# Fourier layer and two expert layers: both halves of an inverse-transform group in one burst at the end of expert steps 1 to 9

## The chip, the cores and the metric

The kernel runs on one core of a Trainium2 chip. Five engines with queues of their own work side by side: TensorE (PE, its weight loads shown as PEld), VectorE (DVE), ScalarE (ACT), GpSimd (POOL) and SyncE (SP, which issues the DMA transfers). Each takes its instructions in the order of its queue, and semaphores hold an instruction back until what it needs is there. The metric is the device time of a run in microseconds (us). The kernel before takes 1156.77 us (median of 3 runs, 1155.72 to 1156.81).

## The reference

Three layers follow each other on two sequences of 3008 tokens with 256 channels:

```python
X = np.fft.rfft(x, axis=1)                       # forward transform along the tokens
Yr = Xr @ w_r - Xi @ w_i + b_r                   # complex product with 256 x 256 weights
Yi = Xr @ w_i + Xi @ w_r + b_i
Yr = sign(Yr) * max(|Yr| - 0.01, 0)              # the same for Yi
y  = np.fft.irfft(Yr + 1j * Yi, n=3008, axis=1)  # inverse transform, 6016 x 256
h = y @ moe_w_in;   g = h * cos(h);              z   = g @ moe_w_out    # 256 -> 2048 -> 256
h = z @ moe2_w_in;  g = h * relu6(h + 3) / 6;    out = g @ moe2_w_out
```

## The kernel before, in words

The first 160 us are the forward transform, the complex product and the shrinking. The inverse transform is cut into 16 groups of 4 token pairs, 376 tokens each; a group has two halves of 128 output channels, and a half (`y_mm`, line 393) is four products of 96 rows, 128 columns of weights (`u_sb`) and 94 columns (`tg_sb`) into one PSUM bank, which the profile counts as 8 matmuls since they are in plain f32. `y_out` (lines 408 and 412) copies the bank to SBUF with ACT and stores it; after the second half it issues the loads of the next group's `u_sb` and `tg_sb`, whose buffers are single. Six groups are done during the transform stage; one follows in the drain of that stage, one half at a time, and the other nine (7 to 15) lie in the expert steps 1 to 9.

The expert layers run in 96 steps (`for k in range(2 * G)`): 6 blocks of up to 1024 tokens times 8 steps for each of the two layers. A step takes two times 128 of the 2048 hidden channels for two halves of the tokens, with the Strassen-Winograd scheme: seven products in place of eight, each product three matmuls of 512 columns (`three`, line 845), since operands are held as a high and a low part. The four results a, b, c and d stand in four PSUM banks with the tags `h0` to `h3`; a is always in `h0` and c always in `h2`. In the order of PE a step is: product A11 into a, an output group, products into c, b, a (A12), an output group, products S3 into b and S4 into d, an output group, product A22 into b, an output group. An output group (`out_mm`) multiplies one finished block's `gh` and `gl` by the output weights and adds into two accumulators, one for each half `d` of the output channels, with three matmuls each. The list `waiting` holds the blocks; the group behind A11 is that of a block of two steps ago.

Between the products stand the elementwise steps of a block (`Block`). In the first layer `first` is an ACT copy to integers (line 820) and a DVE multiply-add that reads the bank (line 821), `second` is ACT's Sin (line 829) and a DVE multiply with the bank as one operand (line 830), and `split` is an ACT copy to `gh` (line 836) and a POOL subtraction to `gl` (line 172). Line 830 is the last reader of a block's bank. DVE also adds into d and c (line 857); the copies of lines 982 and 991 are ACT's. In the steps up to 7 DVE and POOL convert the 64-bit weights of the second layer beside this, one piece at a time, at three places of a step (`other`; lines 199 to 214, 274), and the next block's operands are made with ACT and POOL (`advance`; lines 448 to 454). In steps 2 to 7 and 10 to 15 `advance` also stands between `be.first()` and `bc.second()`.

The order on each engine is the order of the code (manual schedule). What the change touches are `out_mm` and the places of the two halves in a step: the first half is issued behind the third output group into bank `h0` (`y_begin`), its copy comes at once in ACT's order (`y_end`), the second half stands behind A22, also in `h0`, and its copy behind `be.first()`.

Of the kernel before, what the change touches and what calls it, by code (L numbers as in the profile page):

```python
# [9 lines left out]
F32 = mybir.dt.float32  # L10
# [31 lines left out]
STEPS = NFC // 2  # L42
# [80 lines left out]
def fourier_moe_moe_kernel(ctx, tc, x, w_r, w_i, b_r, b_i, ta, tg, fg, win1, wout1, win2, wout2, out):  # L123
# [676 lines left out]
    with tc.manual_schedule(engines=engines):  # L800
# [57 lines left out]

        def out_mm(blk):
            m, jj, q, n = blk.m, blk.jj, blk.q, blk.n  # L860
            f = 4 * (q // 2) + q % 2 + 2 * (1 - blk.f)
            if (jj, blk.t) not in acc:
                acc[jj, blk.t] = [psum.tile([128, 512], F32, tag=f"acc{d}", bufs=2, name=f"acc{jj}_{blk.t}{d}") for d in range(2)]
            w = wo_sb[m, f // 2]
            for d in range(2):
                wz = [w[:, z, f % 2, d * 128 : (d + 1) * 128] for z in range(2)]
                three(acc[jj, blk.t][d], wz, blk.g, q == 0 and blk.f == 0, q == STEPS - 1 and blk.f == 1, n)
            if q == STEPS - 1 and blk.f == 1:
                ended.append((jj, blk.t))
# [81 lines left out]

        def y_begin(tag=None):
            if y_late:
                y_open.append(y_late.pop(0))
                name = f"yp{y_open[0][0]}_{y_open[0][1]}"
                y_mm(*y_open[0], bank(0, name) if tag is None else psum.tile([128, 512], F32, tag=tag, bufs=2, name=name))

        def y_end():
            if y_open:
                y_out(*y_open.pop())  # L960

# [11 lines left out]
        for k in range(2 * G):  # L973
# [4 lines left out]
            def mm(h, w, x, start=False):  # L978
                three(h, weights(k, w), tokens(k, x), start, True, n)

            mm(a, A11, B11, True)
            act.activation(b[:, :n], a[:, :n], AF.Copy)  # L982
            if old:
                od, oe, oc = old
                od.split()
                oe.second()
            drained(k)
            out_next(5)
            mm(c, S1, T1, True)
# [38 lines left out]
            out_next()  # L1028
            if k:
                y_begin()  # L1030
                y_end()
            bd.second()
            if k == 0:
                bc.second()
            mm(b, A22, T4)
            if k:
                y_begin()
            else:
                drained(k)
            be.first()  # L1040
            y_end()
            advance(k, False)
# [4 lines left out]
            other(k, 2)  # L1047
            ba.split()
            flush()
            old = bd, be, bc  # L1050
# [55 lines left out]
```

## Time and profile before

| | |
|---|---|
| median of 3 runs | 1156.77 us |
| span of the profiled execution | 1154.4 us |
| PE busy | 1146.0 us, 99% |
| DVE, ACT, POOL busy | 759.1, 818.3, 805.1 us |
| granted TensorE clock | 1.000 of full speed over the span |
| instructions | 15875 |

The profiled execution's own time is its span: the 1154.4 us from its first to its last instruction. The median of the timed runs is 2.4 us above that. A step's place in the trace is found by its first matmuls into `ha`: steps 1 to 10 begin at 168.01, 181.58, 194.00, 207.01, 219.17, 231.57, 244.85, 256.99, 269.12 and 281.43 us. The rows name tiles without their numbers; `yp` is the bank of a half, `yo` its copy, `ha` to `hd` are the banks of the blocks, `acc` the accumulators. A matmul of 512 columns is shown with 0.39 us, but the next begins 0.22 to 0.23 us after it: matmuls overlap, so starts are compared.

### The profile page before, as it was taken

Reading aid. Unit: us, or ns where it says so; the run is one execution under the profiler, and the core shown is the slowest. Engines: PE = TensorE matmul, PEld = TensorE weight load, DVE = VectorE, ACT = ScalarE, POOL = GpSimd, SP = SyncE. Lnnn points to the kernel's source line nnn. Section 1 sums busy time; section 2 is a strip of 40 time slices with the busy share of each in tenths; the row PEclk is TensorE's granted clock in tenths of the full one; section 3 lists DMA queues with packets and bytes.
Section 4 is the critical chain, followed back from the end, with each engine's and each line's share of the span. In section 5 each row is a group of like instructions: output and inputs, shape, how many; then the busy total and the mean of one; then the engine's idle time right before and its main releaser. Section 6 shows DMA issues by size and latency. Waiting matters only on the chain.

```text
span 1154.4 us, 15875 instructions
## 1 busy us (share of the span) xinstructions
PE 1146.0 (99%) x5345; PEld 961.7 (83%) x5345; DVE 759.1 (66%) x1096; ACT 818.3 (71%) x1561; POOL 805.1 (70%) x650
## 2 busy tenths in 40 slices
PE   9999999999999999999999999999999999999998
PEld 7888877878888888888889987888888888888897
DVE  5888867876988788889886677643443433433443
ACT  5787787777888878888888875565566565556554
POOL 3556747876886996897877776557667667567544
PEclk9999999999999999999999999999999999999999
DMA  9656858435113113112025310020020010100100
GB/s 241 179 149 176 260 173 308 145 109 183 55 37 110 46 55 110 37 73 100 34 63 211 137 69 1 1 74 1 1 73 1 29 45 1 69 1 1 37 1 32
DMA packets 48450, 98.94 MB, mean 86 GB/s; under 512 B 6240, under 2 KB 23184, under 8 KB 47728
## 3 DMA queue, kind: packets, MB, share of 16 engines
q1 hardware_dynamic: 48096, 97.66, 26.3%
q8 instruction: 42, 0.69, 0.2%
q14 instruction: 40, 0.33, 0.1%
q10 hardware_dynamic: 272, 0.26, 0.1%
HBM read 59.76 MB, written 38.14 MB: 85 GB/s over the span
## 4 chain that ended last, share of the span: by engine, by line
PE 95%; DVE 2%; ACT 1%; issue 1%; POOL 1%; DVEq 0%; ACTq 0%; POOLq 0%
PE acc L845 43%; PE hb L845 16%; PE ha L845 11%; PE pp L630 6%; PE hc L845 5%; PE hd L845 5%; PE bp L659 3%; PE yp L393 3%; PE zp L533 2%; PE vp L695 1%; DVE r L830 0%; ACT r L829 0%; POOL x_big L552 0%; POOL tok L451 0%; DVE hd L857 0%
## 5 line engine op out<-in xcount | busy, mean ns | idle before, releaser
L172 POOL TENSOR_TENSOR gl<-r,gh 128x512 fp32r<-128x512 f32 (+1 forms) x382 | 498.1, 1320 | 254.1 <-ACT gh L836 237.6
L845 PE MATMUL acc<-gh,wo 128*128 128x512 f32 (+1 forms) x1536 | 529.5, 386 | 0.0
L845 PEld LDWEIGHTS acc<-gh,wo 128*128 128x128 f32 x1536 | 288.4, 188 | 53.5
L845 PE MATMUL acc<-gl,wo 128*128 128x512 f32 (+1 forms) x768 | 296.3, 386 | 0.0
L845 PE MATMUL hb<-tok,wi 128*128 128x512 f32 (+1 forms) x864 | 241.2, 387 | 2.0 <-ACT hb L982 0.7
L836 ACT ACTIVATE gh<-r 128x512 fp32r<-128x512 f32 (+1 forms) x384 | 227.5, 614 | 1.6 <-DVE r L830 1.2
L845 PEld LDWEIGHTS hb<-tok,wi 128*128 128x128 f32 x864 | 160.9, 188 | 34.0 <-DVE hc L857 1.7
L857 DVE TENSOR_TENSOR hd<-p,hb 128x512 f32<-128x512 f32 (+1 forms) x96 | 65.8, 685 | 159.6 <-PE hb L845 152.6
L845 PEld LDWEIGHTS acc<-gl,wo 128*128 128x128 f32 x768 | 144.2, 188 | 27.8 <-POOL gl L172 1.1
L829 ACT ACTIVATE r<-r 128x512 f32<-128x512 f32 (+1 forms) x192 | 118.7, 618 | 58.4 <-DVE r L821 58.4
L845 PE MATMUL ha<-tok,wi 128*128 128x512 f32 (+1 forms) x576 | 159.8, 386 | 0.0
L845 PEld LDWEIGHTS ha<-tok,wi 128*128 128x128 f32 x576 | 108.0, 188 | 20.5 <-ACT r L829 0.3
L451 POOL TENSOR_TENSOR tok<-st,tok 128x512 fp32r<-128x512 f32 (+1 forms) x77 | 98.6, 1292 | 3.4 <-ACT tok L448 3.4
L991 ACT ACTIVATE p<-hc 128x512 f32<-128x512 f32 (+1 forms) x96 | 56.5, 588 | 54.3 <-PE hc L845 54.1
L823 ACT ACTIVATE r<-hd 128x512 f32<-128x512 f32 (+1 forms) x48 | 28.4, 591 | 78.3 <-PE hd L845 78.3
L845 PE MATMUL hc<-tok,wi 128*128 128x512 f32 (+1 forms) x288 | 79.9, 386 | 0.0
L845 PE MATMUL hd<-tok,wi 128*128 128x512 f32 (+1 forms) x288 | 79.7, 385 | 0.0
L982 ACT ACTIVATE hb<-ha 128x512 f32<-128x512 f32 (+1 forms) x96 | 55.3, 576 | 31.9 <-PE ha L845 31.5
L857 DVE TENSOR_TENSOR hc<-p,hb 128x512 f32<-128x512 f32 (+1 forms) x96 | 65.3, 681 | 16.1 <-PE hb L845 15.3
L845 PEld LDWEIGHTS hc<-tok,wi 128*128 128x128 f32 x288 | 53.9, 188 | 10.5 <-DVE r L830 0.4
L845 PEld LDWEIGHTS hd<-tok,wi 128*128 128x128 f32 x288 | 54.1, 188 | 10.2
L823 ACT ACTIVATE r<-hb 128x512 f32<-128x512 f32 (+1 forms) x48 | 28.3, 590 | 43.9 <-PE hb L845 41.0
(138 smaller groups left out, 1693.8 us busy)
## 6 DMA issues: line engine op xcount, KB each, us to landing
st<-x_dram SPq DMA_DIRECT2D x18, 512.0 KB, 4.7
wi<-wi_dram SPq DMA_DIRECT2D x5, 1792.0 KB, 8.3
rawi<-in_win_dram SPq DMA_DIRECT2D x16, 512.0 KB, 4.0
rawo<-in_wout_dram SPq DMA_DIRECT2D x16, 512.0 KB, 3.7
u_dram<-v SPq DMA_DIRECT2D x48, 128.0 KB, 2.4
u_sb<-u_dram SPq DMA_DIRECT2D x16, 384.0 KB, 3.9
wo<-wo_dram SPq DMA_DIRECT2D x10, 512.0 KB, 6.3
x_dram<-o SPq DMA_DIRECT2D x20, 256.0 KB, 2.3
```

Source lines behind the costliest of these rows:

```text
L172: nc.gpsimd.tensor_tensor(out, x, y, op=ALU.subtract)
L393: pe.matmul(yp[:, i * TP : (i + 1) * TP], lhsT=u_sb[g][:, i, ec * 128 : (ec + 1) * 128], rhs=tg_sb[g][:, i * TP : (i + 1) * TP], start=Tru ...
L451: subtract(at(lo, t), src, f32(at(hi, t)), op=ALU.subtract)
L630: pe.matmul(pp.rearrange("p a e -> p (a e)"), lhsT=za[:, p, kc, 2 * (k2 % 2) : 2 * (k2 % 2) + 2, :].rearrange("p r n -> p (r n)"), rhs=wb[ ...
L659: pe.matmul(bp, lhsT=fgr[:, fi, :], rhs=src[:, :, m, :], start=False, stop=(n == 5), skip_group_check=True)
L823: act.activation(r, h, AF.Relu, bias=3.0, scale=1.0)
L829: act.activation(r, r, AF.Sin, bias=math.pi / 2, scale=1.0)
L836: act.activation(gh[:, :n], self.r[:, :n], AF.Copy)
L845: pe.matmul(h[:, :n], lhsT=w, rhs=x, start=start and j == 0, stop=stop and j == 2, skip_group_check=True)
L857: dve.tensor_tensor(h[:, :n], r[:, :n], x[:, :n], op=ALU.add)
L982: act.activation(b[:, :n], a[:, :n], AF.Copy)
L991: act.activation(p5[:, :n], c[:, :n], AF.Copy)
```

## The change

The two halves of a group are issued together at the end of a step, behind `ba.split()`: the first into `h0` (block a's bank), the second into `h2` (block c's). They are copied at the start of the next step: the first copy, then `od.split()`, which before stood behind the copy of line 982, then the second copy. In steps 2 to 10 the output group that followed A11 is cut in its two halves: the three matmuls for the first 128 channels now come ahead of A11, the other three stay. `y_open` becomes a list with up to two entries, taken from its front.

```diff
--- before.py
+++ after.py
@@ -856,16 +856,16 @@
         def add(h, r, x, n):
             dve.tensor_tensor(h[:, :n], r[:, :n], x[:, :n], op=ALU.add)
 
-        def out_mm(blk):
+        def out_mm(blk, ds=range(2)):
             m, jj, q, n = blk.m, blk.jj, blk.q, blk.n
             f = 4 * (q // 2) + q % 2 + 2 * (1 - blk.f)
             if (jj, blk.t) not in acc:
                 acc[jj, blk.t] = [psum.tile([128, 512], F32, tag=f"acc{d}", bufs=2, name=f"acc{jj}_{blk.t}{d}") for d in range(2)]
             w = wo_sb[m, f // 2]
-            for d in range(2):
+            for d in ds:
                 wz = [w[:, z, f % 2, d * 128 : (d + 1) * 128] for z in range(2)]
                 three(acc[jj, blk.t][d], wz, blk.g, q == 0 and blk.f == 0, q == STEPS - 1 and blk.f == 1, n)
-            if q == STEPS - 1 and blk.f == 1:
+            if q == STEPS - 1 and blk.f == 1 and 1 in ds:
                 ended.append((jj, blk.t))
 
         def finish(jj, t):
@@ -949,15 +949,15 @@
 
         y_open = []
 
-        def y_begin(tag=None):
+        def y_begin(tag=None, z=0):
             if y_late:
                 y_open.append(y_late.pop(0))
-                name = f"yp{y_open[0][0]}_{y_open[0][1]}"
-                y_mm(*y_open[0], bank(0, name) if tag is None else psum.tile([128, 512], F32, tag=tag, bufs=2, name=name))
+                name = f"yp{y_open[-1][0]}_{y_open[-1][1]}"
+                y_mm(*y_open[-1], bank(z, name) if tag is None else psum.tile([128, 512], F32, tag=tag, bufs=2, name=name))
 
         def y_end():
             if y_open:
-                y_out(*y_open.pop())
+                y_out(*y_open.pop(0))
 
         cv.add(1, range(4))
         old, waiting = None, []
@@ -978,14 +978,24 @@
             def mm(h, w, x, start=False):
                 three(h, weights(k, w), tokens(k, x), start, True, n)
 
+            od, oe, oc = old or (None, None, None)
+            halves = [range(2)]
+            if y_open:
+                y_end()
+                od.split()
+                y_end()
+                if len(waiting) >= 5:
+                    halves = [range(1), range(1, 2)]
+                    out_mm(waiting[0], halves.pop(0))
+                od.split = lambda: None
             mm(a, A11, B11, True)
             act.activation(b[:, :n], a[:, :n], AF.Copy)
             if old:
-                od, oe, oc = old
                 od.split()
                 oe.second()
             drained(k)
-            out_next(5)
+            if len(waiting) >= 5:
+                out_mm(waiting.pop(0), *halves)
             mm(c, S1, T1, True)
             p5 = persist.tile([128, 512], F32, tag="r", bufs=5, name=f"p5_{k}")
             act.activation(p5[:, :n], c[:, :n], AF.Copy)
@@ -1026,19 +1036,13 @@
             if k == 0:
                 drained(k)
             out_next()
-            if k:
-                y_begin()
-                y_end()
             bd.second()
             if k == 0:
                 bc.second()
             mm(b, A22, T4)
-            if k:
-                y_begin()
-            else:
+            if k == 0:
                 drained(k)
             be.first()
-            y_end()
             advance(k, False)
             if k:
                 bc.second()
@@ -1046,6 +1050,9 @@
             out_next()
             other(k, 2)
             ba.split()
+            if k:
+                y_begin()
+                y_begin(z=2)
             flush()
             old = bd, be, bc
             waiting += [ba, bd, be, bc]
```

On PE, the end of step 7 and the start of step 8, before (`yp13` is group 13, `_0` and `_1` its halves; `hb_7` is A22, `ha_8` A11 of step 8; a group of output matmuls is cut to its ends):

```order
L845 MATMUL acc0_11_2004<-gh6_01_2699,wo07_2509 128x512
L393 MATMUL yp13_0_2764<-tg_sb13_2674,u_sb13_2672 128x94 x4
L845 MATMUL hb_7_2692<-tok0_1447,wi03_2125 128x512 x3
L393 MATMUL yp13_1_2778<-tg_sb13_2674,u_sb13_2672 128x94 x4
L845 MATMUL acc0_00_1979<-gh6_10_2727,wo06_2362 128x512
...
L845 MATMUL acc0_01_1980<-gh6_10_2727,wo06_2362 128x512
L845 MATMUL ha_8_2809<-tok1_2097,wi00_515 128x512 x3
L845 MATMUL acc0_10_2003<-gh6_11_2716,wo06_2362 128x512
```

and now:

```order
L845 MATMUL acc0_11_2004<-gh6_01_2688,wo07_2509 128x512
L845 MATMUL hb_7_2682<-tok0_1447,wi03_2125 128x512 x3
L845 MATMUL acc0_00_1979<-gh6_10_2727,wo06_2362 128x512
...
L845 MATMUL acc0_01_1980<-gh6_10_2727,wo06_2362 128x512
L393 MATMUL yp13_0_2787<-tg_sb13_2696,u_sb13_2694 128x94 x4
L393 MATMUL yp13_1_2792<-tg_sb13_2696,u_sb13_2694 128x94 x4
L845 MATMUL acc0_10_2003<-gh6_11_2716,wo06_2362 128x512
...
L845 MATMUL ha_8_2797<-tok1_2097,wi00_515 128x512 x3
L845 MATMUL acc0_11_2004<-gh6_11_2716,wo06_2362 128x512
```

The halves stand next to each other, behind the fourth output group, and three output matmuls stand between them and A11.

On ACT, the same place, before (`r7_01`, `r7_10` and `r7_11` are the tiles of blocks d, b and c of step 7, `gh7_00` that of block a):

```order
L820 ACTIVATE r7_11_2755<-hc_7_2693 128x512
L412 ACTIVATE yo13_0_2769<-yp13_0_2764 128x376
L829 ACTIVATE r7_01_2752<-r7_01_2752 128x512
L820 ACTIVATE r7_10_2783<-hb_7_2692 128x512
L412 ACTIVATE yo13_1_2786<-yp13_1_2778 128x376
L829 ACTIVATE r7_11_2755<-r7_11_2755 128x512
L199 ACTIVATE cvao100_2614<-rawo100_2613 128x512
L836 ACTIVATE gh7_00_2805<-r7_00_2733 128x512
L982 ACTIVATE hb_8_2810<-ha_8_2809 128x512
L836 ACTIVATE gh7_01_2817<-r7_01_2752 128x512
```

and now:

```order
L820 ACTIVATE r7_11_2755<-hc_7_2683 128x512
L829 ACTIVATE r7_01_2752<-r7_01_2752 128x512
L820 ACTIVATE r7_10_2769<-hb_7_2682 128x512
L829 ACTIVATE r7_11_2755<-r7_11_2755 128x512
L199 ACTIVATE cvao100_2614<-rawo100_2613 128x512
L836 ACTIVATE gh7_00_2783<-r7_00_2733 128x512
L412 ACTIVATE yo13_0_2801<-yp13_0_2787 128x376
L836 ACTIVATE gh7_01_2805<-r7_01_2752 128x512
L412 ACTIVATE yo13_1_2809<-yp13_1_2792 128x376
L992 ACTIVATE hb_8_2798<-ha_8_2797 128x512
```

The two copies no longer stand between the steps of blocks d, b and c; they stand around `gh7_01`, ahead of the copy into `hb_8`.

On SP, the stores and loads of step 3 (`yo9` is group 9, `u_sb10` and `tg_sb10` the operands of the next), before:

```order
L418 DMA x_dram03_92<-yo9_0_2274 128x376
L382 DMA u_sb10_2292<-u_dram1_64 96x1024
...
L418 DMA x_dram03_92<-yo9_1_2290 128x376
L192 DMA rawi100_2308<-in_win2_dram 128x1024
L903 DMA wo04_2317<-wo_dram04_77 128x1024
L903 DMA wo05_2319<-wo_dram05_78 128x1024
```

and now:

```order
L192 DMA rawi100_2288<-in_win2_dram 128x1024
L903 DMA wo04_2307<-wo_dram04_77 128x1024
L903 DMA wo05_2309<-wo_dram05_78 128x1024
L418 DMA x_dram03_92<-yo9_0_2315 128x376
L382 DMA u_sb10_2324<-u_dram1_64 96x1024
...
L418 DMA x_dram03_92<-yo9_1_2322 128x376
```

The store and the load of group 10 have moved behind the loads of a raw weight and of two output weights.

## Rows read from the trace of the kernel before

**Rows 1.** The page, part 1: busy us (share of the span) and instructions of TensorE.
```profile
PE 1146.0 (99%) x5345; PEld 961.7 (83%) x5345; DVE 759.1 (66%) x1096; ACT 818.3 (71%) x1561; POOL 805.1 (70%) x650
```

**Rows 2.** Windows of steps 2, 7, 9, 10: us, busy (count) by engine, clock, DMA.
```profile
181.58:194.00 12.42, 12.42 (x62) 10.15 (x62) 7.40 (x12) 10.30 (x21) 11.25 (x11) 1.00 0.81 269
...
244.85:256.99 12.14, 12.14 (x63) 10.16 (x62) 10.59 (x14) 8.49 (x17) 9.52 (x7) 1.00 0.29 80
...
269.12:281.43 12.31, 12.31 (x63) 10.08 (x62) 8.76 (x15) 10.33 (x21) 7.82 (x6) 1.00 0.83 280
281.43:291.65 10.22, 10.22 (x47) 8.44 (x46) 7.48 (x11) 8.62 (x18) 8.57 (x7) 1.00 0.53 194
```

**Rows 3.** Timeline of PE, end of step 7: start us, us, engine, line, operation [idle].
```profile
253.01 1.03 PE L393 MATMUL yp<-tg_sb,u_sb 96*128 96x94 f32 x8
253.82 0.94 PE L845 MATMUL hb<-tok,wi 128*128 128x512 f32 x3
254.61 1.13 PE L393 MATMUL yp<-tg_sb,u_sb 96*128 96x94 f32 x8
255.53 0.48 PE L845 MATMUL acc<-gh,wo 128*128 128x512 f32 x1
255.84 0.40 PE L845 MATMUL acc<-gl,wo 128*128 128x512 f32 x1
```

**Rows 4.** Waits of weight loads in steps 1 to 9; timeline around step 6's first half.
```profile
PEld yp L393 <- ACT yo L412: 2.6, 9, 0.3
PEld hb L845 <- DVE hd L857: 1.0, 2, 0.5
...
239.91 0.39 PE L845 MATMUL acc<-gh,wo 128*128 128x512 f32 x1
240.02 0.69 DVE L830 TENSOR_TENSOR r<-r,ha 128x512 f32<-128x512 f32 x1
240.76 1.13 PE L393 MATMUL yp<-tg_sb,u_sb 96*128 96x94 f32 x8 [0.46 <-DVE r L830]
```

**Rows 5.** Timeline of DVE and ACT, end of step 10, and two rows of step 11.
```profile
289.86 0.68 DVE L821 SCALAR_TENSOR_TENSOR r<-r,hd 128x512 f32<-128x512 int32 x1
290.57 0.63 ACT L829 ACTIVATE r<-r 128x512 f32<-128x512 f32 x1 [0.38 <-DVE r L821]
291.24 0.69 DVE L830 TENSOR_TENSOR r<-r,hd 128x512 f32<-128x512 f32 x1
291.84 0.68 DVE L821 SCALAR_TENSOR_TENSOR r<-r,hb 128x512 f32<-128x512 int32 x1
292.11 0.62 ACT L829 ACTIVATE r<-r 128x512 f32<-128x512 f32 x1
292.76 0.69 DVE L830 TENSOR_TENSOR r<-r,hc 128x512 f32<-128x512 f32 x1 [0.24 <-ACT r L829]
...
299.78 0.68 DVE L821 SCALAR_TENSOR_TENSOR r<-r,hd 128x512 f32<-128x512 int32 x1
302.36 0.68 DVE L830 TENSOR_TENSOR r<-r,hc 128x512 f32<-128x512 f32 x1
```

**Rows 6.** Timeline of DVE: L821 on `hd` in steps 1, 7 and 9.
```profile
177.59 0.68 DVE L821 SCALAR_TENSOR_TENSOR r<-r,hd 128x512 f32<-128x512 int32 x1
...
253.48 0.67 DVE L821 SCALAR_TENSOR_TENSOR r<-r,hd 128x512 f32<-128x512 int32 x1
...
277.19 0.68 DVE L821 SCALAR_TENSOR_TENSOR r<-r,hd 128x512 f32<-128x512 int32 x1
```

**Rows 7.** Lines 211 and 214 from 160 to 400 us: duration ns min/median/max, starts.
```profile
L211 DVE TENSOR_SCALAR rawi<-cvai x5: 422/1484/1533, 177.3 to 364.0; 128x512 uint32<-128x512 uint32 x5
L214 DVE SCALAR_TENSOR_TENSOR rawi<-rawi x5: 686/1671/1753, 181.9 to 367.4; 128x512 f32<-128x512 uint32 x5
```

**Rows 8.** The page, part 6 (KB each, us to landing); timeline of SP's queue, step 3.
```profile
u_sb<-u_dram SPq DMA_DIRECT2D x16, 384.0 KB, 3.9
...
208.60 2.02 SPq L903 DMA_DIRECT2D wo<-wo_dram  x2
```

## Prediction

> **What bounds the kernel now.** I read the page first: TensorE (PE) is busy 1146.0 of 1154.4 us, 99% [rows 1]. So a change counts only where it alters what PE issues or lengthens a wait in front of it. Then the windows, one per expert step from its first `ha` matmul to the next one's: steps 2 to 9 run from 181.58 to 281.43 us, 99.85 us in all; step 7 takes 12.14 us, step 10, the first without an inverse-transform pair, 10.22 us for its 45 matmuls of 512 columns, 0.227 us each [rows 2]. A pair costs some 1.92 us. The timeline of PE in step 7 splits that [rows 3]: the first half starts with no idle time before it and occupies 0.81 us (253.01 to 253.82); the three A22 matmuls behind it take 0.79 us, against 3 x 0.227 = 0.68 alone; the second half takes 0.92 us (254.61 to 255.53); the output matmul behind it 0.31 (to 255.84), 0.08 too many. 0.81 + 0.11 + 0.92 + 0.08 = 1.92. Steps 2 to 9 at 12.12 us each would be 97.0 us; so they lose 2.85 us in waits.
>
> The profiled execution has a span of 1154.4 us; the median of the timed runs is 1156.77. I take the difference between the two kernels from the trace and add it to the median.
>
> **The change part by part.** No instruction of PE, ScalarE (ACT), VectorE (DVE) or GpSimd (POOL) is added or removed. The two halves move behind the step's fourth output group, and their copies into the next step.
>
> 1. *The pair without its gaps.* One exit in place of two is 0.11 us a step less: 0.81 + 0.92 + 0.08 = 1.81 us, if the second half waits for its bank and so keeps its 0.92. Nine steps: -1.0 us. In before it takes 0.92 because its weight load waits for the copy of the first half, nine times, 2.6 us in all [rows 4]; in the changed kernel it would wait for another bank's reader (point 3). The Trainium skill (TensorE: Matmul & The Clock Gate, Step-by-step) says that weight loads are pulled ahead of running matmuls; by that rule alone a second half would cost 0.81 and the pairs would give 2.0 instead of 1.0 us. The trace agrees only for halves that wait for nothing.
>
> 2. *The wait for bank h0 goes.* The first half overwrites block a's bank and waits for its last reader, DVE's L830 on `ha`. In step 6 the last output matmul starts at 239.91, the half could start at 240.14 and starts at 240.76 [rows 4]. Read like this, steps 1, 2, 3, 6 and 9 lose 0.39, 0.09, 0.39, 0.62 and 0.05 us, and each of the five halves takes 0.92 for 0.81: 1.54 + 0.55 = 2.1 us. Behind the move that reader has 2.04 us more (three matmuls and the six of an output group, 9 x 0.227), so the wait is gone: -2.1 us. Small waits elsewhere in steps 2, 3, 5 and 6 (read in the same way 0.17, 0.33, 0.24 and 0.37 us; among them are the weight loads that wait for DVE's add into `hd` [rows 4]; with steps 2 to 9 of the waits above they make 2.7 of the 2.85 us) come from DVE, ACT and POOL running late; the stalls of point 3 give these engines time, so I count them as gone too: -1.1 us.
>
> 3. *The new wait: the second half in bank h2.* It may start only when block c has been read for the last time, by L830 on `hc`. Let T be the end of the third output group. PE reaches the second half at T + 0.68 (A22) + 1.36 (fourth output group) + 0.81 (first half) = T + 2.85 us. What stands in front of the reader is seen best in step 10, where no copies of a half lie between [rows 5]: L821 on `hd` starts at 289.86, ACT's Sin for it at 290.57, L830 on `hd` at 291.24, L821 on `hb` at 291.84, the Sin for `hc` only at 292.11, since a copy for the operands runs between, and L830 on `hc` from 292.76 for 0.69 us. From the start of L821 on `hd` (call it D) to the end: 3.59 us with that operand copy; in step 11, without it, 299.78 to 302.36 + 0.68, 3.26 us. DVE to PE takes 0.05 us more (a half started at 240.76 behind a multiply that ended at 240.71). So the second half waits (D - T) + 3.31 - 2.85 = (D - T) + 0.46 us, and 0.33 more in steps 2, 4 and 5, which have the operand copy.
>
> D comes from the trace [rows 6] (three of its nine rows), T from PE's timeline; D lies before the pair in before too, so the move doesn't alter it. D - T for steps 1 to 9: 0.59, 0.90, 1.22, 0.46, 0.37, 1.15, 0.47, -0.47, -0.09 us. Step 7 as an example: 253.48 - 253.01 = 0.47, wait 0.93 us. Steps 8 and 9 are early because only steps 1 to 7 have a piece of weight conversion on DVE between L830 on `ha` and L821 on `hd`. Waits: 1.05, 1.69, 1.68, 1.25, 1.16, 1.61, 0.93, 0.10 (step 8: here the `hb` matmuls, not DVE, set the pace), 0.37: 9.84 us.
>
> Do they heal? D is late for two reasons. In steps 1, 2, 4, 5 and 7 the chain starts from PE itself (add into `hc` as soon as the `hb` matmuls end, then a multiply, the conversion piece, L821), and a stall of PE in the step before shifts all of it. In steps 3 and 6 DVE enters the step late, with two conversion pieces ahead of the add into `hd`; there the changed kernel's `ha` comes 0.92 + 0.68 = 1.6 us behind the end of L830 on `hc`, where in before it came ahead of that end, so that the two pieces are done in time. Following DVE's order from there I get D - T near 0.35 and 0.72, about as in steps 4 and 7. That makes the waits 0.81 and 1.18 us, the sum 8.5 us.
>
> The length of a conversion piece is the soft spot: the same piece at L211 took 0.42 to 1.53 us, at L214 0.69 to 1.75 us [rows 7]. With the shortest in each of steps 3 to 7 the sum falls by some 1.9 us; with 0.4 us more in each of steps 1 to 7, which is still below the longest, it grows by 2.8 us. I take the lengths of before. The Trainium skill (SBUF - State Buffer, Who interferes with whom) says that a VectorE instruction with two SBUF inputs and a GpSimd instruction that reads SBUF shut each other out. The spread of L214, which has two, agrees; by this rule the pieces stretch wherever GpSimd is at work, and a PE stall doesn't change that.
>
> 4. *The copies on ACT.* They stood between ACT's Sin steps and had to wait for PE; now they stand behind `gh` of block a. The next step's first `ha` matmul needs the first copy: PE reaches it one half (0.92) and one half-group (0.68) after the second half starts. In the worst step, 2, I place Sin for `hc` at T + 3.1, two conversion copies, `gh` and the copy behind it at about half a microsecond each, done at T + 5.7, against PE at T + 6.1: hidden by 0.4 us. Were the cover gone, a step would pay the lateness, 0.5 us per ACT instruction in between. The second copy is needed 1.36 us later. Cost: 0.
>
> 5. *Loads and stores on the DMA queue.* A group's `u_sb` load now is issued behind the weight loads of its step, and needed at the end of the next. It lands 3.9 us after issue [rows 8] and has some 9 us, less what the queue holds up: 0.
>
> Sum: 8.5 - 1.0 - 2.1 - 1.1 = +4.3 us. 1156.77 + 4.3 = **1161.1 us**, slower by 0.4%.
>
> **Rivals.**
>
> *The stalls heal.* If every PE stall let DVE arrive relatively earlier in the next step, also where I call the chain driven by PE, the waits would halve to some 4.2 us and cancel the 4.2 us gained: 1156.8. For it: DVE has idle time in these steps. Against it: in steps 4, 5 and 7, where before shows no late start, D - T is still 0.37 to 0.47. Chance 0.16.
>
> *The bank is free in time.* Then the second half takes 0.81, the gain is 2.0 + 2.1 + 1.1 = 5.2 us: 1151.6, faster. It decides where L830 on `hc` ends by T + 2.8, that is D - T of -0.46 or less; step 8 alone of before is there, and seven others are 0.8 us or more away. It needs the conversion pieces to leave their place. Chance 0.08.
>
> *The load of the next group comes late.* Ahead of it on SP now stand the step's raw-weight load, which waits for POOL, and two `wo` loads; of step 3 these are issued from 208.60 to 210.62 in before [rows 8]. Behind them `u_sb` would land at about 214.6, and the burst of step 4 wants it near 217 (later still with the stalls). It decides if the landing takes over 6 us behind the two loads; one or two steps then pay up to 2 us each on top: 1164. Chance 0.06.
>
> The forecast has the remaining 0.70, with a range of its own of 1159 to 1163.5: from the shortest conversion pieces (+2.4) to waits of 9.8 us with none of the small waits healed (9.8 - 1.0 - 2.1 = +6.7).
>
> **How the numbers follow.** 0.2% is 2.3 us, about what a measurement of this kernel can tell from no change. Slower by more (above 1159.1): nine tenths of the forecast and the late load, 0.69. Within: the rest of the forecast and the healing case, 0.23. Faster: 0.08. The range for 8 in 10 takes in the healing case and not the free bank: 1156.6 to 1163.6.
>
> **What would show it.** In the changed profile PE waits in front of the second half, and the releaser is DVE's L830; by step some 1 us in 1 to 7 and next to nothing in 8 and 9. The first halves follow the output group at once. Steps 2 to 9, from `ha` to `ha`, sum to about 103.6 us instead of 99.85; from step 10 on all is as before. I'm wrong if the second half follows 0.81 us behind the first in most steps, if the releaser is ACT or a DMA, or if the difference lies outside steps 1 to 10.

## The result and the profile after

| | before | changed |
|---|---|---|
| median, six runs each | 1156.79 us (1155.72 to 1157.72) | 1163.68 us (1160.96 to 1167.51) |
| span of the profiled execution | 1154.4 us | 1161.2 us |
| PE busy | 1146.0 us | 1147.2 us |
| granted clock over the six runs | 1.000 in the profile | 0.995 to 1.000 |

The ratio is 1.0062, with a 95% interval of 1.0052 to 1.0073: slower, 2.6 us beyond the forecast of 1161.1 us and 0.1 us above the upper end of the range, 1163.6. The six changed runs spread over 6.5 us, against 2.0 before. By their granted clock they took: at 1.000 1160.96 us, at 0.999 1162.64, at 0.998 1163.03 and 1164.33, at 0.997 1166.85, at 0.995 1167.51. The profiled one is that of 1163.03.

Timeline of PE, changed kernel, end of step 7 (answers to [rows 3]); columns are start us, us, engine, line, operation, and in brackets the idle time before it with what ended it:

```profile
261.15 1.03 PE L393 MATMUL yp<-tg_sb,u_sb 96*128 96x94 f32 x8
262.87 1.13 PE L393 MATMUL yp<-tg_sb,u_sb 96*128 96x94 f32 x8 [0.69 <-DVE r L830]
```

The second half starts 1.72 us behind the first; 0.81 is the first half itself, 0.91 the wait for bank h2. DVE in the same step (answers to [rows 6]), with the start of L821 on `hd`, the D of the prediction, and the last reader of bank h2:

```profile
259.56 0.68 DVE L821 SCALAR_TENSOR_TENSOR r<-r,hd 128x512 f32<-128x512 int32 x1
...
262.13 0.68 DVE L830 TENSOR_TENSOR r<-r,hc 128x512 f32<-128x512 f32 x1
```

The reader ends at 262.81, 3.25 us behind D; the prediction had 3.26, and 0.93 us of wait for this step. Read like this, steps 1 to 9 wait 1.06, 1.11, 0.88, 1.01, 1.19, 1.68, 0.91, 0 and 0.38 us: 8.2 us against 8.5 forecast. (These waits are counted between starts; the brackets in the rows, the idle time of PE, are some 0.2 us shorter.) In steps 2 and 4 a part of the wait is hidden: there the first half began 0.59 and 0.24 us late, because its `tg_sb` had not landed (below), and the second half had that much less to wait. Together that is 1.70 and 1.25 us, where the prediction had 1.69 and 1.25. Counted like this the sum is 9.05 us, and the excess over 8.5 is that of step 6, 1.68 for 1.18. In that step DVE stood idle for ACT before a piece of weight conversion, and its L821 on `hd` started 1.4 us behind the end of the third output group, in place of 0.72 (timeline of DVE):

```profile
241.08 1.29 DVE L202 TENSOR_SCALAR cvai<-cvai 128x512 f32<-128x512 f32 x1 [1.30 <-ACT cvai L199]
```

The view of waits (waited for: us in total, times, longest us), changed kernel, answers to [rows 4]:

```profile
PE yp L393 <- DVE r L830: 6.3, 8, 1.5
PE yp L393 <- DMA tg_sb<-in_tg_dram: 0.4, 1, 0.4
...
PEld yp L393 <- DVE r L830: 7.6, 8, 1.6
```

The wait of the weight loads for ACT's copy [rows 4] has left the list; DVE's L830 took its place, and a DMA that the prediction counted as hidden is there too. Windows of the changed kernel, in the columns of [rows 2]: steps 2, 6, 7 and 10 from `ha` to `ha`, then three stretches around the end of step 6:

```profile
182.86:196.60 13.74, 12.49 (x62) 10.23 (x61) 8.83 (x13) 11.58 (x23) 12.54 (x13) 1.00 0.90 328
236.07:250.64 14.57, 13.11 (x62) 10.72 (x61) 11.25 (x14) 9.44 (x18) 10.23 (x8) 0.95 0.38 104
250.64:264.56 13.92, 13.23 (x62) 11.02 (x61) 8.79 (x12) 9.04 (x17) 8.71 (x8) 0.93 0.19 57
289.08:298.63 9.55, 9.55 (x43) 7.88 (x42) 6.36 (x9) 7.26 (x15) 7.21 (x6) 1.00 0.42 153
...
248.00:250.00 2.00, 1.70 (x10) 1.60 (x11) 1.75 (x2) 1.21 (x3) 2.00 (x2) 0.81 0.27 98
250.00:252.00 2.00, 2.00 (x6) 1.52 (x6) 0.00 (x0) 0.02 (x1) 0.89 (x1) 0.50 0.68 147
252.00:254.00 2.00, 2.00 (x9) 1.63 (x8) 0.69 (x1) 1.27 (x3) 0.00 (x0) 0.84 0.66 218
```

The last column but two is the granted clock. Steps 6 and 7 have 0.95 and 0.93, where before had 1.00; inside them the clock is at 0.50, which is 1.2 of 2.4 GHz. (Step 10 is 0.67 us shorter than before only because three output matmuls now stand ahead of its first `ha`.) What PE does there, end of step 6:

```profile
245.81 1.03 PE L393 MATMUL yp<-tg_sb,u_sb 96*128 96x94 f32 x8
248.30 1.20 PE L393 MATMUL yp<-tg_sb,u_sb 96*128 96x94 f32 x8 [1.47 <-DVE r L830]
249.22 0.77 PE L845 MATMUL acc<-gh,wo 128*128 128x512 f32 x1
249.79 0.63 PE L845 MATMUL acc<-gl,wo 128*128 128x512 f32 x1
250.21 0.63 PE L845 MATMUL acc<-gh,wo 128*128 128x512 f32 x1
250.64 1.48 PE L845 MATMUL ha<-tok,wi 128*128 128x512 f32 x3
```

Behind the longest wait of this profile, 1.68 us, matmuls of 512 columns follow each other every 0.43 us in place of 0.227. PE is busy all the while, so no wait is listed: the loss shows only in the clock column. From the clock column it is (1 - 0.81) x 2 + (1 - 0.50) x 2 + (1 - 0.84) x 2 = 1.7 us; the matmuls' starts give 1.6.

The load in step 2, timeline of SP's queue and of PE in the changed kernel:

```profile
183.05 0.45 SPq L384 DMA_DIRECT2D tg_sb<-in_tg_dram  x1
...
185.13 0.33 SPq L899 DMA_DIRECT2D wi<-wi_dram  x1
...
192.99 1.10 PE L393 MATMUL yp<-tg_sb,u_sb 96*128 96x94 f32 x8 [0.43 <-DMA tg_sb<-in_tg_dram]
```

The view of this tile from 178 to 200 us (two loads, issue to landing):

```profile
DMA to landing us min/median/max: 3.9/6.8/9.8
```

In the kernel before, the same `wi` load of 1792 KB left SP at 194.56, since it stood behind the stores of step 2's halves:

```profile
194.56 0.42 SPq L899 DMA_DIRECT2D wi<-wi_dram  x1
```

Now those stores stand behind it, so it leaves 9.4 us earlier and shares the DMA engines with `tg_sb`, which lands 9.8 us after its issue, where the load of this group took 5.1 us before. The `tg_sb` for step 4 is late too: issued at 212.10 behind two `wo` loads, it takes 7.1 us and lands at 219.2, and the first half starts at 219.31, 0.24 us behind its place. Neither late load costs anything by itself here: the second half would have waited for bank h2 until the same moment. (Step 2 takes 13.74 us; in the kernel below whose loads are in time it takes 13.76.)

Steps 2 to 9 took 106.2 us; the prediction said 103.6. Eight steps of 12.03 us without any wait (10.22 us of 512-column matmuls and 1.81 for the pair) are 96.2; the waits for L830 add 7.2, the first halves that were late for `tg_sb` 0.8, the clock 1.7; 0.3 is left, most of it in step 6.

### The profile page after: what moved, and what is told of

Same layout as the page of the kernel before. It is cut to its first block, busy times and chain, and to the rows that moved or that the text cites. A ratio compares the mean times of both kernels' runs of the same rounds, so it can differ in the third digit from the quotient of the medians.

```text
span 1161.2 us, 15862 instructions
## 1 busy us (share of the span) xinstructions
PE 1147.2 (99%) x5345; PEld 965.5 (83%) x5345; DVE 759.7 (65%) x1096; ACT 817.9 (70%) x1561; POOL 805.0 (69%) x650
## 4 chain that ended last, share of the span: by engine, by line
PE 92%; DVE 3%; ACT 2%; POOL 1%; issue 1%; DVEq 0%; POOLq 0%; ACTq 0%
PE acc L845 42%; PE hb L845 15%; PE ha L845 11%; PE pp L630 5%; PE hc L845 5%; PE hd L845 5%; PE bp L659 3%; PE zp L533 2%; PE yp L393 2%; PE vp L695 1%; DVE r L830 1%; DVE r L821 1%; ACT r L829 1%; ACT gh L836 0%; ACT tok L448 0%
## 5 line engine op out<-in xcount | busy, mean ns | idle before, releaser
L830 DVE TENSOR_TENSOR r<-r,hb 128x512 f32<-128x512 f32 (+1 forms) x48 | 32.4, 675 | 53.4 <-ACT r L829 53.2
```

The lines of the kernel that those rows point to most:

```text
L830: dve.tensor_tensor(r, r, self.h[:, : self.n], op=ALU.mult)
```

## Experiments

My theory after this result: the changed kernel pays for the bank as forecast; on top come a fall of the clock behind the longest waits and loads that move in SP's order. Rivals: the time beyond the forecast is something else in the burst of two halves, or DVE as a whole is late. The first four kernels below ran on one chip and the others on a second one; before took 1157.76 us beside the first four, 1157.70 beside the next four and 1157.78 beside the last four, and each ratio is to that.

### Second half in the bank of block d

```diff
-                y_begin(z=2)
+                y_begin(z=3 if k % 2 == 0 else 1)
```

Here a part of the accumulation of the next step's product in that bank isn't done, because the half's matmuls have used it in between; all instructions are there.

> The second half goes into the bank of block d instead of that of block c; nothing else changes. Theory (bank and clock): the loss is the waits of the second half for line 830 on hc, 8.2 us in the changed kernel's trace, and on top of them stretches at half clock behind the longest waits. Line 830 on hd ends 1.2 us earlier, so waits stay only in steps 2 and 6, together under 0.7 us: 1151.5 to 1152.5 us, granted clock 1.000 in every run. Rival (loads): the excess over the sum comes from loads issued behind others, such as the 0.43 us wait for tg_sb in step 2; it stays and grows as steps get shorter: 1153 to 1156. Rival (copies): the copies at the step's start hold PE up: 1160 or more.

Measured 1159.76 us, ratio 1.0018 (1.0005 to 1.0030). The waits for L830 fell to 0.3 us, but the gain did not come. Timeline, PE behind step 2, then SP and PE in step 4:

```profile
195.69 0.96 PE L845 MATMUL ha<-tok,wi 128*128 128x512 f32 x3 [0.87 <-ACT yo L412]
...
208.59 1.92 SPq L903 DMA_DIRECT2D wo<-wo_dram  x2
...
211.51 0.58 SPq L384 DMA_DIRECT2D tg_sb<-in_tg_dram  x1
...
219.75 2.72 PE L393 MATMUL yp<-tg_sb,u_sb 96*128 96x94 f32 x16 [2.21 <-DMA tg_sb<-in_tg_dram]
```

Windows of the same kernel behind that wait:

```profile
220.00:222.00 2.00, 2.00 (x15) 2.00 (x15) 0.33 (x1) 1.00 (x2) 1.93 (x2) 0.71 0.00 0
222.00:224.00 2.00, 2.00 (x7) 1.65 (x7) 0.00 (x0) 0.48 (x1) 1.93 (x2) 0.50 0.63 119
```

My expectation of 1151.5 to 1152.5 us was wrong: with the bank free, the rival of the late load decides step 4 just as the prediction described it, behind two `wo` loads, and the copy on ACT decides step 2. And the clock falls to 0.50 behind a wait for a DMA as well, so it isn't DVE's doing.

### Second half behind half an output group

```diff
 ...
+                out_mm(waiting[0], halves.pop(0))
+                y_open.append(y_late.pop(0))
+                y_mm(*y_open[0], second)
                 y_end()
```

> The three output matmuls that stood behind the burst stand between the two halves, so the second half is wanted 0.68 us later. Theory (bank and clock): each wait is 0.68 us shorter, 8.2 us become about 3.1, and with 0.1 us more per step for a second exit from the small matmuls: 1156 to 1158 us, clock 1.000, since no wait over about 1 us is left. Without a part of the clock (waits cost only their length) the same time, but then the changed kernel's runs at 1.000 and at 0.995 have to differ for another reason. Rival (loads): 1159 or more, a wait for tg_sb in the trace.

Measured 1159.62 us, ratio 1.0022 (1.0009 to 1.0035). The waits for L830 are 1.8 us in all, none above 0.8, and the profiled clock is 1.000, as expected. The time is above the 1156 to 1158 expected, where the rival of the loads had it, and a late load is there:

```profile
219.76 1.10 PE L393 MATMUL yp<-tg_sb,u_sb 96*128 96x94 f32 x8 [1.44 <-DMA tg_sb<-in_tg_dram]
```

In this profile the clock stayed at 1.00 behind that wait. Four of twelve runs had a clock of 0.996 or 0.997 and took 1162.6 to 1163.8 us; the eight at 1.000 took 1156.2 to 1159.7.

### Weight loads behind the stores of the halves

```diff
             if y_open:
                 y_end()
                 ...
+                w_loads(k - 1)
 ...
-            w_loads(k)
+            if not y_open:
+                w_loads(k)
```

> The changed kernel, but the weight loads of a step are issued behind the stores and loads of the halves again, as in the kernel before. Theory (bank and clock): only the 0.43 us of step 2 goes; 1161 to 1164 us, and the clock still differs from run to run, below 1.000 in most. Rival (loads): 1161 or less, and a clock of 1.000 in every run, since the order of the loads was the cause.

Measured 1164.03 us (ratio 1.0053, 1.0041 to 1.0066). No wait for `tg_sb` is left, its landing takes at most 5.4 us, and yet no time is gained that the interval could tell (6.3 us above before, against 6.9): the halves then start earlier and wait longer for the bank. The view of waits:

```profile
PE yp L393 <- DVE r L830: 7.3, 8, 1.5
```

Timeline of PE, end of step 2:

```profile
195.59 1.13 PE L393 MATMUL yp<-tg_sb,u_sb 96*128 96x94 f32 x8 [1.49 <-DVE r L830]
...
197.29 1.40 PE L845 MATMUL ha<-tok,wi 128*128 128x512 f32 x3
```

Step 2, at full clock in the changed kernel, now has the long wait and behind it three matmuls that occupy 1.40 us for 0.84: a fall behind a long wait in another step. A second one stands behind the wait of 1.04 us in step 4, while the wait of 1.48 us in step 6, as long as that of step 2, passed at full clock.

### First half in bank h2, second in h0

```diff
-                y_begin()
-                y_begin(z=2)
+                y_begin(z=2)
+                y_begin()
```

> The first half goes into block c's bank and the second into block a's, so that the wait for line 830 on hc begins 0.81 us earlier in each of nine steps: 8.2 us of waits become about 15.5. Theory with the clock: stretches at half clock behind most of the waits, each some 1.6 us: 1173 to 1183 us, clock 0.995 or less. Waits that cost only their length: 1168.5 us, clock 1.000.

Measured 1175.0 us (ratio 1.0149, 1.0135 to 1.0162), clock 0.996 in the profile. The first half, 0.81 us, no longer covers part of the time to the reader, and the waits double. The view of waits:

```profile
PE yp L393 <- DVE r L830: 14.9, 9, 2.4
```

Timeline of PE, end of step 1, a step that kept its clock in the changed kernel:

```profile
181.10 2.70 PE L393 MATMUL yp<-tg_sb,u_sb 96*128 96x94 f32 x16 [1.72 <-DVE r L830]
...
184.93 1.21 PE L845 MATMUL ha<-tok,wi 128*128 128x512 f32 x3
```

The time is that of the theory with the clock, above the 1168.5 of the one without. But the falls are three, behind steps 1, 2 and 6, and not behind most of the nine waits: those of 1.50, 1.90, 1.85 and 1.57 us in steps 3, 4, 5 and 7 passed at full clock. Timeline of PE, end of step 4:

```profile
227.06 2.02 PE L393 MATMUL yp<-tg_sb,u_sb 96*128 96x94 f32 x16 [1.90 <-DVE r L830]
```

The two halves behind that wait take 2.02 us; behind the wait of step 1 they take 2.70.

### Block c ahead of block d, weight loads behind the stores

```diff
-            bd.first()
+            b1, b2 = (bc, bd) if 1 <= k <= 9 else (bd, bc)
+            b1.first()
```

(and so on with `b2.first()`, `b1.second()`, `b2.second()`; `od.split()` stands behind both `y_end()`.)

> The changed kernel, with two edits: in steps 1 to 9 block c's two passes are issued ahead of block d's (so that the bank of the second half is the first of the two to come free), and the weight loads of a step are issued behind the stores of the halves. Theory (the change gains 5.1 us at its old place and loses the wait for the bank, the late load of tg_sb and the half clock behind the longest waits): the second half's wait for DVE L830 is under 0.3 us in every step, no wait for tg_sb in any step, granted clock 1.000, 1151.5 to 1153.5 us. Rival A (the clock falls for a reason that has nothing to do with the waits, such as the burst of short matmuls of two halves): clock 0.995 to 0.999 with half-clock stretches behind bursts without a wait, 1155 to 1160. Rival B (block d's passes, now late, hold up another product or the next step's copies): a new wait for ACT or DVE on hd or r of block d of 0.5 us or more per step, 1157 to 1161.

Measured 1155.87 us, ratio 0.9982 (0.9973 to 0.9991), clock 0.999 or 1.000 in all runs. The view of waits:

```profile
PE yp L393 <- DVE r L830: 0.5, 2, 0.3
```

Timeline of ACT and PE around the start of step 3:

```profile
193.61 1.14 ACT L274 ACTIVATE wi<-w 128x512 fp32r<-128x512 f32 x2
...
195.17 0.84 ACT L412 ACTIVATE yo<-yp 128x376 f32<-128x376 f32 x2
...
195.69 0.97 PE L845 MATMUL ha<-tok,wi 128*128 128x512 f32 x3 [0.88 <-ACT yo L412]
```

With the order of the loads alone the kernel took 1164.03 us; the rest of the way to 1155.87 is block c's place, with the second copy ahead of `od.split()`: it turns the change from a loss into a gain. Rival A is out: nine bursts stand there, without a long wait, and no run is below 0.999. It is faster than before by 1.8 us, not at the 1151.5 to 1153.5 expected: 0.9 us of the missing are the copy `yo`, late behind two copies of weights on ACT (0.4 us of cover in the prediction held only as long as PE stalled), and the small waits don't heal when nothing stalls: steps 7 to 9 take 12.03 to 12.05 us, but step 2 13.47, step 4 12.35 and step 6 12.78. Over steps 2 to 9 the waits are 2.8 us, about as many as the 2.85 of before. Timeline of PE, end of step 3, a burst that waits for nothing:

```profile
205.36 1.92 PE L393 MATMUL yp<-tg_sb,u_sb 96*128 96x94 f32 x16
207.07 0.47 PE L845 MATMUL acc<-gh,wo 128*128 128x512 f32 x1
```

It takes 1.70 us, not twice 0.81: the second half costs 0.89 us with its bank free, and the pair the same 1.8 us as with a wait, its length apart.

### Bank of block d with the weight loads behind the stores

> The second half in the bank of block d (which is free before the step ends) and the weight loads of a step behind the stores of the halves; as in the run with the bank of block d alone, a part of the next step's accumulation into that bank is not done. Theory: no wait for L830 above 0.3 us, no wait for tg_sb, clock 1.000, 1151.5 to 1153.5 us (0.9 of which is for the wait for yo in step 2, if it stays). Rival A (clock for another reason): dips without waits, 1155 to 1160. Rival C (the queue's order was not what held tg_sb back): the wait of 2.2 us for tg_sb in step 4 stays, 1157 to 1160.

The edits of the first and the third run together. Measured 1155.65 us, ratio 0.9986 (0.9977 to 0.9994), clock 1.000. No wait for `tg_sb` is left, so SP's order was its cause; the time is 4.1 us less than with the bank of block d alone, on the other chip, a part of it the half clock that most runs of that kernel had. As in the kernel above, 0.9 us go to `yo` in step 2, and the gain is 2.1 us, less than half of what I expected.

### Half an output group between, weight loads behind the stores

> The second half begins only behind three output matmuls of the next step, and the weight loads of a step are issued behind the stores of the halves. Theory: the waits for L830 stay at about 1.8 us in three or four steps (0.76 at most in one), the 1.4 us wait for tg_sb goes, clock 1.000 in most runs: 1154.5 to 1157. Rival C (the queue's order is not the cause): the wait for tg_sb stays, 1158 to 1160, as without the second edit.

Measured 1157.98 us, ratio 1.0000 (0.9991 to 1.0009), clock 1.000 in all eleven runs: the load's wait is gone, the waits for L830 are 2.1 us, none above 0.8. That is 1 us above the range expected. No run lost clock, though PE waited for L830 four times.

### One single long wait

```diff
-                y_begin()
-                y_begin(z=3 if k % 2 == 0 else 1)
+                y_begin(z=2 if k == 6 else 0)
+                y_begin(z=0 if k == 6 else 3 if k % 2 == 0 else 1)
```

> The kernel with the second half in the bank of block d and the weight loads behind the stores, but in step 6 the first half goes to block c's bank and the second to block b's old one, so that one single wait of 2.0 to 2.6 us for L830 stands at the end of step 6 and none elsewhere. It changes the same part of the accumulation as the kernel with the bank of block d. Theory (a wait of this length brings the clock to half for some 3 us, which costs 1.6 us more): the profile or most runs show a granted clock of 0.996 to 0.999, a stretch at 0.50 behind the wait, and the time is that of the kernel without the wait plus 3.5 to 4.3 us. Rival A (the clock has nothing to do with the wait): clock as in the kernel without it, plus 2.0 to 2.6 us only.

The edit puts the second half of step 6 into block a's bank, h0; "block b's old one" in the expectation is a slip. Measured 1159.54 us, 3.9 us above the same kernel without the wait (1155.65), inside the 3.5 to 4.3 expected; rival A had 2.0 to 2.6. Timeline of PE, end of step 6:

```profile
245.26 2.41 PE L393 MATMUL yp<-tg_sb,u_sb 96*128 96x94 f32 x16 [2.33 <-DVE r L830]
```

Windows of the same kernel there:

```profile
246.00:248.00 2.00, 2.00 (x14) 1.90 (x14) 0.70 (x1) 1.30 (x3) 0.60 (x2) 0.68 0.11 39
248.00:250.00 2.00, 2.00 (x6) 1.60 (x5) 0.00 (x0) 0.18 (x1) 0.84 (x1) 0.50 0.73 166
250.00:252.00 2.00, 2.00 (x10) 1.58 (x9) 0.53 (x1) 1.42 (x3) 0.00 (x0) 0.96 0.83 252
```

A long wait put there alone, and a fall of the clock right behind it: 0.64 + 1.00 + 0.08 = 1.7 us, the price it had in the changed kernel. In the two profiles steps 6 and 7 are 28.5 us in place of 24.8. Not every run has the fall: three of the eleven had a clock of 1.000 and took 1157.5 to 1158.8 us, 1.9 to 3.1 above 1155.65, about the length of the wait alone. The Trainium skill (TensorE: Matmul & The Clock Gate, A second HAM failure mode: psum-queue depth-cycling) tells of a kernel whose PE idles briefly and often between groups of matmuls and swings between the two rates. This trace shows the same swing, 1.00, 0.50 and back, around a single wait of 2.33 us.

### The conversion piece behind the reader of block c

```diff
-            other(k, 1)
+            if not 1 <= k <= 9:
+                other(k, 1)
 ...
                 bc.second()
+            if 1 <= k <= 9:
+                other(k, 1)
```

(on top of the weight loads behind the stores)

> The changed kernel with the weight loads of a step behind the stores of the halves, and in steps 1 to 9 the piece of weight conversion that stands on DVE between L830 on ha and L821 on hd moved behind L830 on hc. Theory (that piece, 0.6 to 1.5 us in steps 1 to 7, is what makes L830 on hc late): the waits of the second half for L830 fall from 8.2 us to 1 to 4 us, none above 1.2 us, granted clock 0.999 to 1.000, 1155 to 1159 us. Rival (DVE as a whole is late, whatever the order): the wait moves to the add into hd or to ha's multiply at the next step's start, waits in front of hb, ha or the halves add up to 6 us or more, 1161 to 1165.

Measured 1157.98 us, ratio 1.0000 (0.9991 to 1.0009), clock 1.000 in all eleven runs. Waits:

```profile
PE yp L393 <- DVE r L830: 2.5, 6, 0.7
```

From 7.3 us, in the kernel with the weight loads behind the stores alone, to 2.5 by the place of one DVE piece a step; the time is inside the 1155 to 1159 expected, and the rival, that DVE is late whatever the order, is out. This is the soft spot that the prediction named.

### The changed kernel again

> The changed kernel once more, unaltered, for the spread of its runs and their clocks beside the others of this call. Theory of the clock: its runs at 1.000 stand within 1 us of 1161, the forecast, and each 0.001 that the clock is lower adds about 1.2 us (a granted clock of half over 2 us of the span); the median 1162.5 to 1164. Rival (the spread has nothing to do with the clock): no relation between time and clock over the runs.

Measured 1167.43 us (1163.92 to 1170.0, six runs), ratio 1.0079 (1.0063 to 1.0095). Runs by clock: 0.994: 1170.0 and 1168.5; 0.995: 1167.7; 0.997: 1167.2; 0.998: 1163.9; 1.000: 1164.5. The profiled one, 0.994, has three falls, behind the waits at the ends of steps 2, 4 and 6, with a longest wait of 1.9 us; the middle one is the longest:

```profile
224.00:226.00 2.00, 2.00 (x11) 2.00 (x11) 0.12 (x1) 1.00 (x2) 2.00 (x2) 0.50 0.00 0
226.00:228.00 2.00, 2.00 (x7) 1.61 (x7) 0.00 (x0) 0.48 (x1) 1.72 (x2) 0.50 0.75 156
228.00:230.00 2.00, 2.00 (x7) 1.52 (x6) 0.00 (x0) 1.05 (x2) 0.00 (x0) 0.50 1.02 386
```

The trend is there, but two parts of the expectation failed: the median is above 1162.5 to 1164, and the run at 1.000 lies 3.4 us above 1161, not within 1. The waits vary too (8.2 us for PE in this profile, 6.3 in the first), and the kernel before was 1 us slower beside these runs than beside the first. The longest wait is that of step 4, and it stands in front of the first half (timeline of PE):

```profile
223.22 3.08 PE L393 MATMUL yp<-tg_sb,u_sb 96*128 96x94 f32 x16 [1.88 <-DVE r L830]
```

The row puts it down to L830, but the first half needs bank h0, whose reader L830 on `ha` ended at 218.97. Its `tg_sb` was issued at 214.42 and landed 8.7 us later, at 223.1. So a late load can cost the changed kernel more than in the first profile: the first half starts only when the second could have, some 0.9 us lost, and the longest fall of the clock stands behind it. How long these loads take to land (7.1 and 8.7 us in step 4, 9.8 and 7.6 in step 2) is one of the things that differ between the two profiles.

### Block c ahead of block d, once more

> The kernel with block c ahead of block d and the weight loads behind the stores once more, for comparison on the same chip: 1155 to 1156.5, 1.5 to 2 us below the kernel before, clock 1.000.

Measured 1155.63 us, ratio 0.9983 (0.9974 to 0.9992): the gain repeats.

### The copies of the halves ahead of a piece of conversion

```diff
-                cv.step(1 + (place == 2 and k < 6))
+                cv.step(1 + (place == 2 and k < 6 and not (1 <= k <= 5)))
 ...
                 oe.second()
+            if behind:
+                if 2 <= k <= 6:
+                    cv.step(1)
+                w_loads(k - 1)
```

(on top of block c ahead of block d; `behind` is true where halves were stored.)

> The kernel with block c ahead of block d and the weight loads behind the stores, with one more edit: of the two pieces of weight conversion at the end of steps 1 to 5 the second is issued only in the next step, behind the two copies of the halves and the copy into hb. Theory (with the wait for the bank gone, the copy of the first half on ACT is what ends last in step 2, 0.88 us): no wait of ha for yo L412 above 0.4 us, 0.5 to 1.0 us faster than without the edit on the same chip, clock 1.000, 1154 to 1155.5. Rival (the conversion is late now, and POOL or DVE with it): the 0.88 us come back as another wait, no difference of more than 0.4 us.

Measured 1155.02 us, ratio 0.9974 (0.9965 to 0.9983), 0.6 us below the kernel it builds on (1155.63); the intervals of the two overlap. The view of waits:

```profile
PE ha L845 <- ACT yo L412: 0.4, 1, 0.4
```

Windows of steps 2 and 9:

```profile
182.75:195.66 12.91, 12.52 (x61) 10.20 (x61) 7.65 (x13) 10.58 (x21) 10.86 (x11) 1.00 0.67 233
269.06:281.10 12.04, 12.04 (x63) 10.23 (x61) 8.41 (x13) 10.03 (x20) 7.65 (x6) 1.00 0.95 292
```

Step 2 was 13.46 us without the edit. A new wait of 0.5 us for the load of `wi` stands in front of step 2 in this profile; no run shows whether the edit causes it. This is the fastest version: 2.8 us faster than before, over 12 us faster than the changed kernel on the same chip. Step 9 is at the 12.03 us that the prediction's pair (1.81) gives.

## Why the prediction was right and wrong

- **Direction and mechanism: right.** PE waits in front of the second half, the releaser is L830, some 1 us in steps 1 to 7 and next to nothing in 8 and 9, as point 3 had it. Its sum, 8.5 us, measured 8.2, or 9.05 with the 0.8 us that late loads hid in steps 2 and 4. Three runs (the order of the banks, of blocks c and d, of the conversion piece) moved it by about the amounts its mechanism gives. Step by step it holds within 0.1 us but for step 6 (1.68 for 1.18): there the pieces were not done in time as the prediction had it, DVE waited 1.30 us for ACT.
- **The sum: the step that failed.** It added waits as if each cost its own length. A term was missing: behind a long wait PE can run at half clock, 1.7 us each time, with one such fall in the first profile, three in the second (one of them 3.4 us), none in some runs. Shown by the single wait put into a kernel without any (3.9 us for 2.3), whose runs at full clock paid about the length alone. In the first six runs this term is most of the 2.6 us: the run at 1.000 took 1160.96 us, and if from each run the share of its time that the clock lost is taken off, they come to 1160.7 to 1163.4 us, 1161.7 in the mean (an estimate from their clocks), against 1161.1 forecast. The forecast's own range, 1159 to 1163.5, had no term for it either, so its upper end was too low. That the median lies 0.1 us outside the range for 8 in 10 is chance; in the second set of runs it is 3.8 us.
- **Point 1, the pair: the number right, the reason not.** Steps without waits take 12.03 to 12.05 us in the runs with a free bank, 10.22 + 1.81. But the second half costs 0.89 us there although it waits for nothing, so its 0.92 in before is not, but for 0.03, due to the wait for the copy. The 0.81 that the prediction gives a half without a wait holds for the first of two. The free bank was therefore worth 1.0 us at this point, not 2.0.
- **Point 2, waits gone: in the main.** No half waits for bank h0 in the changed kernel's profiles. Of the small waits (-1.1 us) some 0.3 stayed. With the bank free, where PE doesn't stall, some of them are back.
- **Point 5, loads at 0: right in the first profile by luck.** Two loads were late, by 0.59 and 0.24 us, which the wait for the bank covered. In the second profile one cost some 0.9 us, and 1.4 to 2.2 us of waits stand in two experiments. I treated the late load as a rival of 0.06; it is no alternative to the bank's wait but stands beside it, and takes over when that shrinks. Step 4 went as that rival had it, with a landing of 7.1 and 8.7 us behind two `wo` loads; step 2, where the moved stores let a large load run ahead, is not in the prediction.
- **Point 4, copies at 0: right for this kernel**, and only because the stall covers them: 0.9 us in step 2 once it is gone.
- **The rivals.** The stalls did not heal. The free bank, reached by putting block c first, is faster as that rival said, but by 1.8 to 2.2 us (2.8 with the copies) and not by 5.2: 1.0 of the difference is the second half's 0.89, the rest are waits that the bank's wait had covered.
- **Steps 2 to 9.** The prediction's 103.6 us are 103.8 by its own terms; it measured 106.2. Of the 2.5 us between, 1.7 are the clock and 0.5 is step 6.

## What to carry to other kernels

When work is moved to a bank whose last reader comes later, first ask whether the reader can be issued earlier: with the order of two blocks and of the loads changed, 7 us lost became 2 us won. On a PE that is 99% busy, price a wait of more than a microsecond at its length and, as a second term with a chance of its own, the half-clock stretch behind it. When a store moves, follow what stood behind it on its queue: a large load that was held back by it now competes with the small one that is needed next.

## What the runs showed of the hardware

In the profiles here the granted clock fell to 0.50 behind 11 of the 18 waits of PE above 1 us in the expert steps (idle time of 1.03 to 2.36 us, in brackets in the rows), for DVE and for DMA waits alike, and behind no shorter one; the longest without a fall behind it was 1.90 us, the shortest with one 1.04. A fall cost 1.7 us, once 3.4. What decides between two waits of equal length stays open. In a stream of matmuls of 94 columns the second eight take 0.89 us, the first eight behind matmuls of 512 columns 0.81. A 141 KB load took 9.8 us to land with a 1792 KB load issued 2 us after it; in the kernel before, where that one came 9.4 us later, it took 5.1.
